# Attention and two MoE layers in one kernel: scores in quarter tiles, mask on VectorE, one ScalarE pass for PReLU, a reordered prologue with filler matmuls

## The chip, the cores and the metric

The kernel runs on one NeuronCore of one Trainium2 chip. The metric is the device time of one execution in microseconds (us); lower is better. Engine names are those of the profile: PE is TensorE (matmuls), PEld its weight loads, DVE is VectorE, ACT ScalarE, POOL GpSimd, SP the engine whose queue issues the loads.

## The reference

Three stages follow each other on 2304 tokens (4 sequences of 576).

```python
scores = scale * q @ k.T                      # 8 heads of 64, window of 64 keys, causal
mask = (rel >= 0) & (rel < 64)
scores = where(mask, scores, -1e9); attn = softmax(scores); x = attn @ v
h = x @ w_in                                  # 512 -> 2048
g = maximum(h, 0) + alpha * minimum(h, 0)     # PReLU, one alpha per column
x = g @ w_out                                 # 2048 -> 512
e = argmax(x @ w_gate); out = gate * relu(x @ w1[e]) @ w2[e]   # 8 experts, one per token
```

All matrix products have float32 accuracy: the large ones split each operand into a high part that one fast pass takes exactly (type fp32r) and a low remainder, and sum three products (high·high, low·high, high·low).

## The kernel before

**Attention.** 18 tiles of 128 tokens with two halves of 4 heads each make 36 groups `g`. A group goes through these steps, each a function and a letter of the table `PLAN`: `X` loads its queries, keys and values (704 KB); `S` (`qk`) computes the scores; `x` (`mx`) takes the row maximum and scales it on DVE; `e` (`ex`) takes four exponentials of 128 columns on ACT with their row sums; `r`, `n` normalize on DVE; `T` transposes on PE; `P` copies the transposed block out of PSUM on ACT; `O` (`pv`) multiplies by the values; `H` and `L` write the high part (ACT) and low part (DVE) of the result, the input of the next stage. Within a tile a query attends to at most 128 keys per half tile of 64 queries. `qk` uses a block layout: four matmuls (one per head) of 128 rows by 128 columns, in which the stationary operand holds the two half tiles of queries in the two diagonal 64 by 64 blocks and zeros elsewhere. The scores fill one PSUM bank of 4 × 128 columns, and the mask is added on PE: two bf16 matmuls of the identity with a table of 0 and -3e38 (`masks`) open the accumulation.

**PReLU layer (MoE 1).** The tokens form 5 blocks, of 4, 4, 4, 3 and 3 tiles, and the 2048 columns 16 chunks `f`. For each block and chunk: `s` (`s1`, 12 matmuls of 512 columns in the blocks of four tiles) gives `h` in PSUM; ACT makes `relu(h)` in a tile `g` (`act_pos`, letter `g`) and `relu(-h)` in place in PSUM (`act_neg`, `R`); DVE combines them to `g - alpha * relu(-h)` (`act_sum`, `t`); ACT and DVE split the result (`h`, `l`); `u` (`s2`, 12 matmuls) accumulates into one PSUM bank per tile (`acc0` to `acc3`). The weights come as raw 1 MB loads, one per chunk (`W`, `load_w`), from 64-bit words and are converted once: steps `0` (ACT), `1`, `2`, `3` (DVE), `4` (ACT), `5` (DVE).

**Routing and experts.** Rows of the finished block are dotted with the gate (`Z`, `N`, `D`), ranked (`G`, `J`, `j`, `M`) and entered into a list (`I`, `i`); afterwards 20 to 25 slots of 128 tokens run through their expert.

**Order.** From the start to the end of the fourth block the order is written by hand in `PLAN` (line 29): a sequence of tokens, letter and number, that `play` turns into instructions. Every engine executes its instructions in that order, so an instruction that waits holds all behind it on the same engine. Groups 0 to 7 (block 0) come first, in the prologue, with their scores in the banks `acc0` to `acc3`; then `s0` begins the steady state, in which groups 8 to 15 run between the chunks of block 0, groups 16 to 23 between those of block 1, and so on. From group 8 on `S`, `T`, `O` and the routing share two rotating banks, tag `att`. Loads go through SP in order, at most eight at a time in flight.

The scores in the code before:

```python
for a in range(2):
    PE.matmul(out=b[:, 2 * a:2 * a + 2, :], lhsT=ident16, rhs=masks(g), start=(a == 0), stop=False)
for u in range(4):
    a, e = divmod(u, 2)
    PE.matmul(out=b[:, u, :], lhsT=q[:, u, :], rhs=k[:, a, 64 * e:64 * e + 128], start=False, stop=(u == 3))
```

Of the kernel before, what the change touches and what calls it, by code (L numbers as in the profile page):

```python
# [42 lines left out]
g18 R18 D9 t18 u17 D10 h18 D11 x17 N4 s20 l18 e17 D12 D13 D14 u18 g19 r17 R19 n17 t19 D15 h19 T17 D16 N5 S18 P17 l19
O17 D17 g20 u19 R20 D18 X19 H17 t20 L17 h20 D19 s21 l20 N6 x18 D20 e18 u20 D21 D22 D23 g21 r18 R21 N7 n18 s22 t21 D24
h21 D25 T18 l21 S19 P18 D26 g22 D27 O18 R22 x19 u21 H18 X20 t22 e19 L18 D28 s23 D29 h22 r19 l22 n19 u22 D30 g23 R23
D31 t23 G0 h23 T19 s24 P19 O19 l23 J0 H19 X21 u23 j0 g24 R24 s25 L19 t24 S20 M0 h24 s26 l24 x20 g25 R25 e20 t25 u24
h25 r20 n20 I0 S21 l25 M1 g26 u25 R26 t26 x21 h26 e21 I1 l26 s27 i0 r21 n21 T20 g27 u26 P20 R27 t27 h27 O20 l27 T21
H20 X22 u27 P21 L20 O21 S22 H21 X23 L21 s28 x22 e22 s29 g28 r22 n22 R28 t28 T22 S23 P22 h28 O22 x23 s30 l28 H22 X24
e23 L22 u28 g29 r23 n23 R29 t29 h29 T23 s31 l29 P23 g30 R30 t30 u29 h30 O23 l30 S24 g31 X25 H23 u30 x24 R31 L23 e24
t31 s32 h31 r24 n24 l31 u31 g32 R32 t32 h32 s33 Z4 l32 Z5 N8 Z6 N9 Z7 u32 g33 R33 D32 D33 D34 T24 D35 s34 P24 t33 N10  # L50
D36 h33 D37 O24 l33 D38 s35 g34 X26 H24 D39 R34 D40 N11 L24 u33 t34 D41 h34 D42 D43 S25 l34 N12 s36 D44 g35 R35 D45
t35 D46 h35 u34 D47 x25 N13 D48 e25 s37 D49 l35 D50 g36 r25 R36 u35 n25 t36 D51 h36 D52 N14 T25 D53 s38 P25 l36 D54
g37 R37 D55 t37 O25 N15 D56 h37 u36 X27 H25 D57 D58 L25 S26 l37 D59 g38 u37 R38 x26 t38 e26 D60 s39 D61 D62 h38 r26
l38 s40 n26 g39 D63 R39 t39 G1 h39 u38 T26 S27 P26 l39 g40 O26 x27 R40 u39 t40 H26 X28 e27 L26 J1 s41 h40 j1 s42 l40
# [26 lines left out]
def attn_moe_moe_kernel(  # L81
# [22 lines left out]

    def f32(ap):
        return ap.bitcast(FP32)
# [19 lines left out]
    nalpha = const.tile([128, 16], FP32, name="nalpha")  # L126
# [5 lines left out]
    def load_consts(i):  # L132
        if i == 0:
            SP.dma_start(out=c16, in_=cst16.bitcast(BF16))
            return
        SP.dma_start(out=c[:, 0:C_I128], in_=cst[:, 0:C_I128])
        SP.dma_start(out=c[:, C_I128:], in_=cst[:, C_DESC:])

    def prep_consts():
# [5 lines left out]
        DVE.tensor_scalar(out=nalpha, in0=alpha, scalar1=-1.0, scalar2=None, op0=ALU.mult)  # L145
# [66 lines left out]

    xt = {}
# [20 lines left out]
    def abank(g=NBT * 2):  # L234
        return bank(f"acc{g % 4}", 1) if g < 2 * BLOCKS[0][1] else bank("att", 2)

    def masks(g):
        i = g // 2
        if (2 * i) % 9 == 0:
            return c16[:, 4:6, :]  # L240
        if (2 * i + 1) % 9 == 0:
            return c16[:, 3:5, :]
        return c16[:, 3, :].unsqueeze(1).to_broadcast([128, 2, 128])

    def qk(g):
        q = raw[g][:, 0:512].rearrange("p (u q) -> p u q", u=4)
        k = raw[g][:, 512:896].rearrange("p (a k) -> p a k", a=2)
        b = abank(g).rearrange("p (u k) -> p u k", u=4)
        for a in range(2):
            PE.matmul(out=b[:, 2 * a:2 * a + 2, :], lhsT=ident16, rhs=masks(g), start=(a == 0), stop=False)  # L250
# [277 lines left out]
    def r_list(j, h=0):  # L528
        n = BLOCKS[j][1]
        if h == 0:  # L530
            lbs[j] = rbank(j)
# [475 lines left out]
```

## Time and profile before

| what | value |
|---|---|
| median of 3 runs | 794.11 us (793.66 to 794.26) |
| the profiled execution | 793.48 us, its span 791.7 us |
| PE busy | 760.3 us, 96% of the span |
| DVE busy | 609.9 us, 77% |
| ACT busy | 496.2 us, 63% |
| POOL busy | 63.5 us, 8% |
| mean granted PE clock | 0.988 of full |

The span runs from the first to the last instruction; 1.8 us of the execution lie outside it. Busy times are for engines that work at the same time, so they don't add up. A PE that is nearly always busy means that its own instruction stream sets the time in those stretches; the stretches where it isn't are to be looked at one by one. In the timeline a row gives the modelled length of a matmul; the distance from start to start tells what it costs in a stream.

### The profile page before, as it was taken

Reading aid. Unit: us, or ns where it says so; the run is one execution under the profiler, and the core shown is the slowest. Engines: PE = TensorE matmul, PEld = TensorE weight load, DVE = VectorE, ACT = ScalarE, POOL = GpSimd, SP = SyncE. Lnnn points to the kernel's source line nnn. Section 1 sums busy time; section 2 is a strip of 40 time slices with the busy share of each in tenths; the row PEclk is TensorE's granted clock in tenths of the full one; section 3 lists DMA queues with packets and bytes.
Section 4 is the critical chain, followed back from the end, with each engine's and each line's share of the span. In section 5 each row is a group of like instructions: output and inputs, shape, how many; then the busy total and the mean of one; then the engine's idle time right before and its main releaser. Section 6 shows DMA issues by size and latency. Waiting matters only on the chain.

```text
span 791.7 us, 12097 instructions
## 1 busy us (share of the span) xinstructions
PE 760.3 (96%) x4284; PEld 634.6 (80%) x4284; DVE 609.9 (77%) x1210; ACT 496.2 (63%) x966; POOL 63.5 (8%) x50
## 2 busy tenths in 40 slices
PE   5589999999999999999999999999999999999995
PEld 4468888888888888888888889887778888888884
DVE  5699898488544786535885486689999999999997
ACT  4687656535344534335354434587888998989986
POOL 0000000000000000000000001011222221221222
PEclk9879999999999999999999999999999999999998
DMA  9981432223221323112222123532066157767521
GB/s 365 407 325 43 144 114 87 74 77 112 93 72 57 98 70 121 38 37 80 87 88 91 67 78 127 222 127 74 27 235 271 54 190 314 237 265 255 192 87 49
DMA packets 24256, 109.86 MB, mean 139 GB/s; under 512 B 3006, under 2 KB 3390, under 8 KB 17024
## 3 DMA queue, kind: packets, MB, share of 16 engines
q1 hardware_dynamic: 20672, 98.25, 34.1%
q0 software_dynamic: 3520, 10.80, 4.0%
q8 instruction: 35, 0.57, 0.3%
q14 instruction: 29, 0.24, 0.1%
HBM read 154.09 MB, written 10.26 MB: 208 GB/s over the span
## 4 chain that ended last, share of the span: by engine, by line
PE 85%; DVE 7%; DMA 5%; issue 2%; ACT 0%; SPq 0%; DVEq 0%; ACTq 0%
PE acc L700 11%; PE h L336 9%; PE acc L383 9%; PE h L338 8%; PE h L337 8%; PE acc L384 8%; PE acc L385 8%; PE h L672 4%; PE h L674 4%; PE h L673 4%; DVE hl L784 4%; PE att L253 3%; PE att L312 2%; DMA hl<-in_wcat_dram 2%; DMA hl<-in_qkv_dram 2%
## 5 line engine op out<-in xcount | busy, mean ns | idle before, releaser
L784 DVE TENSOR_TENSOR hl<-hl,hl 128x1024 fp32r<-128x1024 f32 x176 | 211.2, 1223 | 14.8 <-ACT hl L778 14.1
L778 ACT CAST hl<-hl 128x1024 fp32r<-128x1024 f32 x176 | 180.3, 1049 | 3.9 <-DMA hl<-in_wx_dram 2.3
L700 PE MATMUL acc<-hl,xl 128*128 128x512 f32 x504 | 130.7, 400 | 2.4 <-DVE xl L687 2.4
L336 PE MATMUL h<-xh,hl 128*128 128x512 f32 (+1 forms) x320 | 121.3, 379 | 0.0
L338 PE MATMUL h<-xh,hl 128*128 128x512 f32 (+1 forms) x320 | 118.1, 369 | 0.0
L337 PE MATMUL h<-xl,hl 128*128 128x512 f32 (+1 forms) x320 | 117.8, 368 | 0.0
L384 PE MATMUL acc<-hl,gl 128*128 128x512 f32 x288 | 112.8, 392 | 0.0
L385 PE MATMUL acc<-hl,gh 128*128 128x512 f32 x288 | 112.8, 392 | 0.0
L383 PE MATMUL acc<-hl,gh 128*128 128x512 f32 x288 | 109.9, 401 | 0.1
L700 PEld LDWEIGHTS acc<-hl,xl 128*128 128x128 f32 x504 | 91.2, 188 | 21.4 <-DVE xl L687 3.7
L354 ACT ACTIVATE g<-h 128x512 f32<-128x512 f32 (+1 forms) x80 | 44.5, 557 | 93.3 <-DVE gl L365 57.9
L648 POOL DMA_INDIRECT gx<-x1d,ixg x23 | 39.8, 1729 | 712.5 <-PE acc L385 486.6
L365 DVE TENSOR_TENSOR gl<-g,gh 128x512 fp32r<-128x512 f32 (+1 forms) x80 | 50.9, 636 | 48.4 <-PE acc L384 39.9
L358 DVE SCALAR_TENSOR_TENSOR g<-h,nalpha,g 128x512 f32<-128x512 f32 (+1 forms) x80 | 55.6, 695 | 39.0 <-ACT h L351 38.9
L298 ACT CAST gh<-g 128x512 fp32r<-128x512 f32 (+1 forms) x80 | 46.3, 579 | 58.3 <-DVE g L358 55.2
L439 DVE SCALAR_TENSOR_TENSOR dot<-stage,wge 128x512 bf16<-128x512 f32 x96 | 66.0, 688 | 2.1
L672 PE MATMUL h<-hl,xh 128*128 128x512 f32 x168 | 67.6, 403 | 0.0
L336 PEld LDWEIGHTS h<-xh,hl 128*128 128x128 f32 x320 | 60.3, 188 | 8.6 <-DVE g L358 0.3
L337 PEld LDWEIGHTS h<-xl,hl 128*128 128x128 f32 x320 | 60.3, 189 | 7.8
L338 PEld LDWEIGHTS h<-xh,hl 128*128 128x128 f32 x320 | 60.1, 188 | 7.9
L674 PE MATMUL h<-hl,xh 128*128 128x512 f32 x168 | 66.0, 393 | 0.3 <-DVE xh L660 0.2
L673 PE MATMUL h<-hl,xh 128*128 128x512 f32 x168 | 65.5, 390 | 0.0
(171 smaller groups left out, 1141.2 us busy)
## 6 DMA issues: line engine op xcount, KB each, us to landing
hl<-in_wx_dram SPq DMA_DIRECT2D x92, 1024.0 KB
raw<-in_qkv_dram SPq DMA_DIRECT2D x31, 704.0 KB
hl<-in_wcat_dram SPq DMA_DIRECT2D x14, 1024.0 KB
wge<-in_wgt_dram SPq DMA_DIRECT2D x24, 256.0 KB
hl<-in_qkv_dram SPq DMA_DIRECT2D x5, 704.0 KB
x1d<-stage SPq DMA_DIRECT2D x3, 1032.0 KB
x<-in_wcat_dram SPq DMA_DIRECT2D x2, 1024.0 KB
gx<-in_wgt_dram SPq DMA_DIRECT2D x8, 256.0 KB
```

The costliest lines, as they stand in the source:

```text
L336: PE.matmul(out=h[:, 0:n], lhsT=w_in_op(f, k, 0), rhs=xh[:, k, :], start=(k == 0), stop=False)
L337: PE.matmul(out=h[:, 0:n], lhsT=w_in_op(f, k, 0), rhs=xl[:, k, :], start=False, stop=False)
L338: PE.matmul(out=h[:, 0:n], lhsT=w_in_op(f, k, 1), rhs=xh[:, k, :], start=False, stop=(k == 3))
L383: PE.matmul(out=a, lhsT=gh[:, c0:c0 + 128], rhs=w_out_op(f, 0), start=(f == 0), stop=False)
L384: PE.matmul(out=a, lhsT=gl[:, c0:c0 + 128], rhs=w_out_op(f, 0), start=False, stop=False)
L385: PE.matmul(out=a, lhsT=gh[:, c0:c0 + 128], rhs=w_out_op(f, 1), start=False, stop=(f == 15))
L672: PE.matmul(out=o, lhsT=th[:, k, :], rhs=wh, start=(k == 0), stop=False)
L673: PE.matmul(out=o, lhsT=th[:, k, :], rhs=wl, start=False, stop=False)
L674: PE.matmul(out=o, lhsT=tl[:, k, :], rhs=wh, start=False, stop=(k == 3))
L700: PE.matmul(out=o, lhsT=x[:, f % 4, :], rhs=w[:, lo, (f % 2) * 512:(f % 2) * 512 + 512], start=(x is th and f == 0 and lo == 0), stop=(x i ...
L778: ACT.copy(out=t[:, 0, :], in_=r)
L784: eng.tensor_tensor(out=t[:, 1, :], in0=r, in1=f32(t[:, 0, :]), op=ALU.subtract)
```

## The change

- **Scores in quarter tiles.** `qk` issues eight matmuls of 64 rows (contraction) by 64 output rows by 128 columns instead of four full ones: for each head pair `a` and each `e`, one per half tile `r`, on the four quadrants of the array in turn. The two half tiles write to two PSUM banks, 256 columns of each. Groups 0 to 7 use pairs of `acc` banks. From group 8 on a group's scores take both `att` banks, which are now handed out by a list (`aslot`, `give`): scores give them back after the exponentials, transposes after `P`, values after `L`.
- **Mask.** Groups 0 to 15 keep the mask as two bf16 matmuls, one per bank. From group 16 on (`LATE`, 20 half tiles) DVE adds it in PSUM before the maximum, two instructions of 256 columns.
- **Small steps.** The maximum is two reductions; its scaling (`y`) and the addition of 1e-9 to the sums (`q`) are steps of their own, on POOL where the token ends in `p` (the groups 2 to 15), else on DVE. Six `P` copies of the prologue go to DVE (`P0d` to `P5d`), three normalizations (`n8a` to `n10a`) to ACT.
- **PReLU.** `act_pos` is gone. ACT writes `relu(-h)` to the tile `g`, and DVE computes `g * (1 - alpha) + h` with `h` from PSUM.
- **Prologue.** A new `PLAN`; tokens `b` and `B` issue filler matmuls on bf16 data (8 on zeros, 47 on the constants, 512 columns each) whose results are not read.
- **Lists.** `r_list` closes its accumulation for each pair of tiles, each followed by its own `r_add`.

```diff
 PLAN = """
-c0 X0 W0 S0 c1 X1 x0 e0 10 X2 C0 00 r0 W1 S1 n0 20 T0 P0 S2 x1 X3 30 O0 e1 x2 X4 11 H0 r1 W2 n1 e2 S3 L0 T1 x3 S4 P1
...
+c0 X0 b8 X1 c1 S0 X2 B2 x0 S1 y0 C0 e0 W0 B7 x1 y1 e1 S2 q0 r0 X3 n0 x2 T0 B2 P0d y2p X4 00 q1 O0 r1 n1 e2 10 T1 X5 S3
...
+    attb = [bank("att0", 1), bank("att1", 1)]
+    idle = [0, 1]
+    held = {}
+    def aslot(who):
+        i = idle.pop(0)
+        held.setdefault(who, []).append(i)
+        return attb[i]
+    def give(who):
+        idle.extend(held.pop(who, []))
...
+    LATE = 2 * BLOCKS[2][0]
...
+    def busy(n, x=None):
+        x = c16[:, 0:4, :].rearrange("p a b -> p (a b)") if x is None else x
+        b = bank("h", 2)
+        for _ in range(n):
+            PE.matmul(out=b, lhsT=x[:, 0:128], rhs=x, start=True, stop=True)
...
-        for a in range(2):
-            PE.matmul(out=b[:, 2 * a:2 * a + 2, :], lhsT=ident16, rhs=masks(g), start=(a == 0), stop=False)
-        for u in range(4):
-            a, e = divmod(u, 2)
-            PE.matmul(out=b[:, u, :], lhsT=q[:, u, :], rhs=k[:, a, 64 * e:64 * e + 128], start=False, stop=(u == 3))
+        if g < 2 * BLOCKS[0][1]:
+            two = [bank(f"acc{2 * (g % 2) + r}", 1) for r in range(2)]
+        else:
+            two = [aslot(("S", g)) for r in range(2)]
+        b = [z[:, 0:256].rearrange("p (a k) -> p a k", a=2) for z in two]
+        added = g >= LATE
+        for r in range(0 if added else 2):
+            PE.matmul(out=b[r], lhsT=ident16, rhs=masks(g).unsqueeze(1).to_broadcast([128, 2, 128]),
+                      start=True, stop=False)
+        for a in range(2):
+            for e in range(2):
+                for r in range(2):
+                    h = slice(64 * r, 64 * r + 64)
+                    PE.matmul(out=b[r][64 * e:64 * e + 64, a, :], lhsT=q[h, 2 * a + e, h], rhs=k[h, a, 64 * e:64 * e + 128],
+                              start=added, stop=(added or a == 1))
...
-        DVE.tensor_reduce(out=nm, in_=sm[g], axis=AX.X, op=ALU.max, negate=True)
-        DVE.tensor_scalar(out=nm, in0=nm, scalar1=0.125, scalar2=None, op0=ALU.mult)
+        for r in range(2):
+            if g >= LATE:
+                m = masks(g).unsqueeze(1).to_broadcast([128, 2, 128])
+                DVE.tensor_tensor(out=sm[g][r], in0=sm[g][r], in1=m, op=ALU.add)
+        for r in range(2):
+            DVE.tensor_reduce(out=nm[:, r, :], in_=sm[g][r], axis=AX.X, op=ALU.max, negate=True)
...
-        ACT.activation(out=hb[j, f], in_=hb[j, f], func=ACTF.Relu, scale=-1.0)
...
-        DVE.scalar_tensor_tensor(out=g, in0=hb.pop((j, f)), scalar=nalpha[:, f:f + 1], in1=g,
-                                 op0=ALU.mult, op1=ALU.add)
+        ACT.activation(out=g_tile(j, f, "g"), in_=hb[j, f], func=ACTF.Relu, scale=-1.0)
...
+        DVE.scalar_tensor_tensor(out=g, in0=g, scalar=beta[:, f:f + 1], in1=hb.pop((j, f)), op0=ALU.mult, op1=ALU.add)
```

The order of instructions shows two places. On PE, the scores of group 16, early in block 1, between the matmuls of `u` and `s` (names are output<-inputs, rows by columns of the output). Before:

```order
L250 LDWEIGHTS c_68
L250 MATMUL att<-c_68 128x256
L250 LDWEIGHTS c_68
L250 MATMUL att<-c_68 128x256
L253 MATMUL att<-raw 128x128 x4
```

Now:

```order
L279 MATMUL att_67<-raw 64x128
L279 MATMUL att_68<-raw 64x128
L279 MATMUL att_67<-raw 64x128
L279 MATMUL att_68<-raw 64x128
L279 MATMUL att_67<-raw 64x128
L279 MATMUL att_68<-raw 64x128
L279 MATMUL att_67<-raw 64x128
L279 MATMUL att_68<-raw 64x128
```

The two mask matmuls are gone, and eight quarter matmuls alternate between the two banks `att_67` and `att_68`.

On DVE, the prologue from the maximum of group 7 on: `L180` (after the change `L195`) is step `1` of a weight chunk, the first instruction of DVE that needs its load, and `hl_288`, `hl_317`, `hl_367` are chunks 3, 4 and 5. Before:

```order
L258 TENSOR_REDUCE nm<-acc_307 128x4
L259 TENSOR_SCALAR nm<-nm 128x4
L180 TENSOR_SCALAR hl_288<-hl_288 128x1024
L275 TENSOR_SCALAR rs<-ss 128x4
L276 RECIPROCAL rs<-rs 128x4
L325 TENSOR_TENSOR xl<-att,xh 128x2x128
L280 TENSOR_TENSOR sm<-sm,rs 128x512
L180 TENSOR_SCALAR hl_317<-hl_317 128x1024
L196 TENSOR_TENSOR hl_355<-hl_95,hl_355 128x2x512
L275 TENSOR_SCALAR rs<-ss 128x4
L276 RECIPROCAL rs<-rs 128x4
```

Now, with `hl_257` and `hl_352` the chunks 1 and 2:

```order
L290 TENSOR_REDUCE nm<-acc_435 128x2
L290 TENSOR_REDUCE nm<-acc_436 128x2
L364 TENSOR_TENSOR xl<-att_68,xh 128x2x128
L337 COPY pt<-att_67 128x512
L313 RECIPROCAL rs<-rs 128x4
L321 TENSOR_TENSOR sm<-sm,rs 128x512
L195 TENSOR_SCALAR hl_257<-hl_257 128x1024
L199 SCALAR_TENSOR_TENSOR hl_257<-hl_257 128x1024
L203 SCALAR_TENSOR_TENSOR hl_257<-hl_257 128x1024
L364 TENSOR_TENSOR xl<-att_68,xh 128x2x128
L313 RECIPROCAL rs<-rs 128x4
L321 TENSOR_TENSOR sm<-sm,rs 128x512
```

Up to the low part `L` of group 7 (the eighth `L325`, now the eighth `L364`) DVE had seven instructions of step `1` ahead, for chunks 0 to 6, and nine of the steps `2`, `3`, `5`; now it has three of step `1`, for chunks 0 to 2, and eight of the others.

## Rows read from the trace of the kernel before

**Rows 1.** Page, the span and part 1 (us, share, instructions).

```profile
span 791.7 us, 12097 instructions
...
PE 760.3 (96%) x4284; PEld 634.6 (80%) x4284; DVE 609.9 (77%) x1210; ACT 496.2 (63%) x966; POOL 63.5 (8%) x50
```

**Rows 2.** By stretch: its length, busy us of each engine, PEclk, DMA share, GB/s.

```profile
0.00:48.10 48.10, 28.33 (x251) 23.16 (x252) 32.12 (x69) 28.59 (x91) 0.40 (x6) 0.86 0.94 372
40.00:50.00 10.00, 6.53 (x41) 5.53 (x40) 9.85 (x14) 8.54 (x10) 0.00 (x0) 0.58 0.79 298
300.00:400.00 100.00, 100.00 (x596) 85.33 (x596) 58.31 (x160) 43.79 (x124) 0.00 (x0) 1.00 0.22 73
```

**Rows 3.** Waits of PE after 48 us: total us, times, longest us.

```profile
PE acc L700 <- DVE xl L687: 2.4, 3, 1.4
```

**Rows 4.** Chain of waits, 0 to 60 us (start us, us, what).

```profile
22.59 15.38 DMA hl<-in_wcat_dram
...
37.99 0.69 DVE hl L180
```

**Rows 5.** Timeline of PE, start of the program (start us, us).

```profile
5.81 2.08 PE L253 MATMUL acc<-raw 128*128 128x128 f32 x8 [1.93 <-DMA raw<-in_qkv_dram]
...
28.82 1.16 PE L253 MATMUL acc<-raw 128*128 128x128 f32 x8 [1.53 <-DMA raw<-in_qkv_dram]
...
47.71 0.77 PE L336 MATMUL h<-xh,hl 128*128 128x512 f32 x1
...
48.55 0.39 PE L338 MATMUL h<-xh,hl 128*128 128x512 f32 x1
```

**Rows 6.** Timeline of PE, scores of group 9 between block-0 matmuls.

```profile
53.34 0.39 PE L338 MATMUL h<-xh,hl 128*128 128x512 f32 x1
53.56 0.39 PE L250 MATMUL att<-c 128*128 128x256 bf16 x2
53.79 1.06 PE L253 MATMUL att<-raw 128*128 128x128 f32 x8
54.61 0.47 PE L336 MATMUL h<-xh,hl 128*128 128x512 f32 x1
54.92 0.39 PE L337 MATMUL h<-xl,hl 128*128 128x512 f32 x1
```

**Rows 7.** Timeline of PE, probabilities times values of group 8.

```profile
71.30 0.39 PE L385 MATMUL acc<-hl,gh 128*128 128x512 f32 x1
71.61 0.69 PE L312 MATMUL att<-pt,raw 128*64 128x64 f32 x16
72.23 0.50 PE L336 MATMUL h<-xh,hl 128*128 128x512 f32 x1
72.56 0.39 PE L337 MATMUL h<-xl,hl 128*128 128x512 f32 x1
```

**Rows 8.** DVE instructions by line, 0 to 48.1 us (busy us, mean ns).

```profile
L280 DVE TENSOR_TENSOR sm<-sm,rs 128x512 f32<-128x512 f32 x8 | 5.5, 691 | 0.4
L258 DVE TENSOR_REDUCE nm<-acc 128x4 f32<-128x512 f32 x8 | 5.5, 689 | 12.3 <-PE acc L253 12.2
L184 DVE SCALAR_TENSOR_TENSOR hl<-hl 128x1024 int32<-128x1024 int32 x4 | 4.9, 1222 | 0.0
L180 DVE TENSOR_SCALAR hl<-hl 128x1024 int32<-128x1024 int32 x7 | 4.8, 691 | 2.2 <-DMA hl<-in_wcat_dram 2.2
...
L325 DVE TENSOR_TENSOR xl<-att,xh 128x256 fp32r<-128x256 f32 x8 | 3.3, 415 | 0.0
...
L259 DVE TENSOR_SCALAR nm<-nm 128x4 f32<-128x4 f32 x8 | 1.4, 170 | 0.3
```

**Rows 9.** Timeline of DVE, the last low part before the steady state.

```profile
47.89 0.42 DVE L325 TENSOR_TENSOR xl<-att,xh 128x256 fp32r<-128x256 f32 x1
```

**Rows 10.** Timeline of ACT, exponentials of group 0 and what follows them.

```profile
8.92 0.37 ACT L267 ACTIVATE sm<-acc,nm 128x128 f32<-128x128 f32 x1 [6.67 <-DVE nm L259]
...
10.31 1.14 ACT L176 ACTIVATE hl<-hl 128x1024 f32<-128x1024 f32 x1
```

More of the change, by code (lines that the diff above doesn't have):

```diff
@@ L134, in load_consts @@
             SP.dma_start(out=c16, in_=cst16.bitcast(BF16))
+            DVE.tensor_copy(out=c16[0:64, 5, :], in_=c16[0:64, 4, :])
+            DVE.tensor_copy(out=c16[0:64, 4, :], in_=c16[0:64, 3, :])
             return
@@ L137, in load_consts @@
         SP.dma_start(out=c[:, C_I128:], in_=cst[:, C_DESC:])
+        POOL.tensor_scalar(out=beta, in0=alpha, scalar1=-1.0, scalar2=1.0, op0=ALU.mult, op1=ALU.add)
     def prep_consts():
@@ L266, in ex, with add_eps @@
         for h in range(4):
-            ACT.activation(out=s[:, h, :], in_=x[:, h, :], func=ACTF.Exp, bias=nm[:, h:h + 1], scale=0.125,
+            ACT.activation(out=s[:, h, :], in_=x[h // 2][:, h % 2, :], func=ACTF.Exp, bias=nm[:, h:h + 1], scale=0.125,
                            accum_out=ss[:, h:h + 1])
+        give(("S", g))
         sm[g] = s
         nrm[g] = ss
+    def add_eps(g, eng=DVE):
+        rs = att.tile([128, 4], FP32, tag="rs", bufs=3, name="rs")
+        eng.tensor_scalar(out=rs, in0=nrm[g], scalar1=1e-9, scalar2=None, op0=ALU.add)
+        nrm[g] = rs
     def recip(g):
-        ss = nrm[g]
-        rs = att.tile([128, 4], FP32, tag="rs", bufs=3, name="rs")
-        DVE.tensor_scalar(out=rs, in0=ss, scalar1=1e-9, scalar2=None, op0=ALU.add)
-        DVE.reciprocal(out=rs, in_=rs)
-        nrm[g] = rs
-    def norm(g, eng=DVE):
-        eng.tensor_tensor(out=sm[g], in0=sm[g], in1=nrm.pop(g).unsqueeze(2).to_broadcast([128, 4, 128]), op=ALU.mult)
+        DVE.reciprocal(out=nrm[g], in_=nrm[g])
+    def norm(g, eng=DVE):
+        s, rs = sm[g], nrm.pop(g)
+        if eng is ACT:
+            for h in range(4):
+                ACT.activation(out=s[:, h, :], in_=s[:, h, :], func=ACTF.Copy, scale=rs[:, h:h + 1])
+            return
+        eng.tensor_tensor(out=s, in0=s, in1=rs.unsqueeze(2).to_broadcast([128, 4, 128]), op=ALU.mult)
     def trans(g):
         s = sm.pop(g)
-        b = bank("att", 2)
+        b = aslot(("T", g))
         for h in range(4):
             PE.transpose(b[:, h * 128:h * 128 + 128], s[:, h, :], ident)
-        pT[g] = b.rearrange("p (u q) -> p u q", u=4)
+        pT[g] = b
     def trans_out(g, eng=ACT):
         t = att.tile([128, 4, 128], FP32, tag="pt", bufs=2, name="pt")
-        copy(eng, t, pT[g])
+        copy(eng, t.rearrange("p h q -> p (h q)"), pT[g])
+        give(("T", g))
         pT[g] = t
     def copy(eng, out, in_):
-        if eng is POOL:
-            POOL.tensor_tensor(out=out, in0=in_, in1=one32.unsqueeze(2).to_broadcast(list(in_.shape)), op=ALU.mult)
-            return
         (eng.copy if eng is ACT else eng.tensor_copy)(out=out, in_=in_)
@@ L399, in rbank @@
     def rbank(j):
-        return pbank("att") if j >= NB - 1 else bank("att", 2)
+        return pbank("att") if j >= NB - 1 else aslot(("R", j))
     def r_trans(j, t, tag="xs"):
@@ L493, in r_place @@
         DVE.tensor_tensor(out=rr, in0=rk, in1=oh, op=ALU.mult)
+        give(("R", j))
         rf = small("m", [])
@@ L528, in r_list @@
     def r_list(j, h=0):
-        n = BLOCKS[j][1]
-        if h == 0:
-            lbs[j] = rbank(j)
-        for t, a, bm in ab.pop(j):
-            PE.matmul(out=lbs[j][:, 0:NCOL], lhsT=bm, rhs=a, start=(t == 0), stop=(t == n - 1))
+        lbs[j] = rbank(j)
+        some = ab.pop(j)
+        for i, (t, a, bm) in enumerate(some):
+            PE.matmul(out=lbs[j][:, 0:NCOL], lhsT=bm, rhs=a, start=(i == 0), stop=(i == len(some) - 1))
     lbs = {}
@@ L566, in small @@
             return e2.tile([128] + shape, dt, bufs=1, tag=own, name=nm, **pad)
-        b = pbank("att") if part else bank("att", 2)
+        b = pbank("att") if part else aslot(("R", NB))
         PE.matmul(out=b[:, 0:NE], lhsT=one16, rhs=ohsum, start=True, stop=True)
@@ L574, in slot_table @@
         DVE.tensor_copy(out=nb, in_=ni)
+        give(("R", NB))
         yield
@@ L815, in attn_moe_moe_kernel @@
     with tc.manual_schedule():
+        POOL.memset(zero16, 0.0)
         POOL.memset(one32, 1.0)
```

117 lines of the change are left out of this document (57 added, 60 removed).

## Prediction

> **What bounds the kernel now.** I first read the page: the span is 791.7 us and PE is busy for 760.3 of it, 96% [rows 1]. So nearly everywhere the PE stream itself sets the time, and the question is where it does not. The busy times by stretch answer that: from 300 to 400 us PE is busy all 100 us, DVE 58.31 and ACT 43.79, while in the first 48.1 us PE has 28.33 [rows 2]. PE's waits after 48 us come to little: the longest kind is 2.4 us in three waits [rows 3]. Two things can therefore be won: PE time anywhere after the prologue, at its full worth, and an earlier start of the steady state.
>
> What bounds the prologue? Its chain of waits is a string of loads up to 38 us; the last, 15.38 us from 22.59 on, is that of weight chunk 5, on which step `1` of that chunk (the DVE piece at 37.99) waits and holds all of DVE behind it [rows 4]. The timeline of PE gives the ends: scores of group 0 at 5.81, those of group 7 at 28.82 (after its load), the first matmul of `s0` at 47.71, and at 48.55 the third one, from which on PE doesn't stop [rows 5]. The clock granted between 40 and 50 us is 0.58 of full [rows 2], so the first matmuls of `s0` run slowly too. Counted at full speed (227 ns from start to start, below), `s0` in effect began at 48.55 - 2 × 0.227 = 48.1 us, with the scores of group 8 already behind it.
>
> The profiled execution took 793.5 us, 0.6 below the median of the runs shown, 794.1. The sum is made against the profile and 0.6 added at the end. A measurement of this kernel can tell about 0.2%, 1.6 us, from no change.
>
> **Scores of a group, in the steady state.** One group before: the last `s` matmul starts at 53.34 and costs 0.227, so scores begin at 53.56; the mask takes until 53.79; the next stream matmul but one starts at 54.92, so the whole ends at 54.92 - 0.23 = 54.69 [rows 6]. That is 1.13 us, 0.23 of it mask and 0.90 the eight passes of four matmuls, 0.113 a pass of 128 columns.
>
> For quarter matmuls the trace of before has no row. The nearest is `O`, which already uses the array in column halves: it runs from 71.30 + 0.227 = 71.53 to 72.56 - 0.23 = 72.33, 0.80 us [rows 7]. Its 16 passes have 64 columns, half of 0.113, so one after another they would need 0.90; they start within 72.23 - 71.61 = 0.62. So the two column halves work at the same time: 8 × 0.056 = 0.45 us, and the other 0.35 is what entering and leaving the split array costs. Bounds for the new scores, 16 passes of 128 columns:
> - only column halves overlap: 8 × 0.113 + 0.35 = 1.25 us;
> - all four quadrants overlap: 4 × 0.113 + 0.35 = 0.80 us.
>
> Nothing in the rows excludes that row halves overlap as column halves do, and the change puts them on separate banks, so that the two writes don't meet; I take 0.80 and keep 1.25 as a rival. The Trainium skill (TensorEngine Tiling (Array Packing), Tiling Modes) lists a 64 by 64 split as four tiles that load weights and multiply independently; by that the lower value holds and the sum below is 782, by the pairs alone that these rows show it is 795. No row here shows four at once.
>
> - Groups 16 to 35, without mask on PE: 1.13 - 0.80 = 0.33 each, 20 × 0.33 = **-6.6 us**.
> - Groups 8 to 15, with the mask (0.23): 1.13 - 1.03 = 0.10 each, **-0.8 us**.
>
> **What hides the rest.** The mask on DVE is two instructions of 256 columns at about 0.415 (the low part `L`, from PSUM, has that size), with the split maximum about 1.0 us more per group on an engine that is busy 58 of 100 us [rows 8, 2]: less than eight groups in that stretch bring it to about 66%, so it costs nothing unless someone waits for it. ACT loses a pass of `h` per chunk; nothing on PE waits for ACT there, so it gains nothing by itself; it shortens the way from `s` to `u`. The lists' extra additions are small DVE work, covered by PE. The fillers only matter where they stand in front of something due: 47 × 0.227 = 10.7 us of PE at full clock, in a prologue where PE has 48.1 - 28.3 = 19.8 us to spare [rows 2]; 32 of them (7.3 us) stand between the scores of group 7 and `s0`, up to seven in a row (1.6 us). That could delay `s0` by up to 3 us, and goes into the range. In return the clock stays up, which is in the 48.1 above.
>
> **The prologue.** DVE is the engine to count. Up to the end of the last `L` of block 0 (47.89 + 0.42 = 48.31 [rows 9]) it is busy 32.12 + 0.21 = 32.3 us and idle 16.0: 7.9 before its first maximum, which follows the scores of group 0 (5.81 + 2.08 [rows 5]), and 8.1 afterwards, of which 12.3 - 7.9 = 4.4 on scores and 2.2 on weight loads [rows 8]. By the order of instructions its work ahead of that `L` changes so, with the means of rows 8:
> - four steps `1` fewer, 4 × 0.691, and one of the long steps fewer, 1.22: -4.0;
> - six scalings and six additions to POOL, 12 × 0.17: -2.0;
> - the maximum in two halves, at 2 × 0.415 instead of 0.689, eight times: +1.1;
> - six copies of `P`, 512 columns, as 0.691 of `n`: +4.1; small constants +0.2.
>
> Together -0.6: the work stays 31.7 us. What goes is waiting: chunks 3 to 5 are no longer asked of DVE before `s0`, and group 7 is loaded before chunk 2. With quarter scores the first maximum can start at about 7.0 (half of the 2.08 saved, at the low clock). If DVE never idled again the last `L` would end at 7.0 + 31.7 = 38.7; with all 8.1 us of idle it would be 46.8. I take 2.5 us of idle, nearer the first, since the loads were the chain's main part: 41.2. `s0` began 0.6 before the end of that `L`; so 40.6, say 41.0 with a filler in front. The scores of group 8 now come after it, 1.03, so the point to set beside 48.1 is 42.0: **-6.1 us**, between -9.0 and -0.9. POOL's small steps have no row of their kind: as cheap as DVE's 0.17 at the best, and at the worst the two of group 7, which nothing covers, add some 3 us, inside the same bounds.
>
> **Two banks for one group.** Between the scores of a group from 8 on and the end of its exponentials neither the next scores nor a transpose can start. The way through is two masks and two maxima (4 × 0.415), a scaling of 0.17 and four exponentials, 10.31 - 8.92 = 1.39 us [rows 10]: 3.2 us. Between the scores of group 17 and the transposes of group 16 the new plan has `s19` and `u17`, 24 × 0.227 = 5.45 us. That leaves 2.2 us for whatever stands ahead on DVE and ACT. I take 28 groups × 0.05 = **+1.5 us** of PE standing; bounds 0 and the rival below.
>
> **Sum:** -6.6 - 0.8 - 6.1 + 1.5 = -12.0: 793.5 - 12.0 = 781.5, and with the 0.6 of the median **782.1 us**.
>
> **Rivals.**
> - *Quarters overlap only in pairs.* Then a group costs 1.25 (groups 16 to 35: +0.12 × 20 = +2.4) or 1.48 with the mask (8 × 0.35 = +2.8), with the prologue and the standing as above: +0.6, 794.7 us. For it: rows 7 show pairs and no more. Against: nothing ties the row halves. Chance 0.15.
> - *The change makes PE wait for the two banks (slower).* Place: between scores and the next transposes or scores in blocks 0 to 3. Price: 28 groups × w on top of -13.5; it decides the sign from w = 0.54 us (over +1.6) and at w = 0.8 gives +8.9, 803.0 us. For it: only 2.2 us of reserve in queues that carry five other kinds of work, and the exponentials, which free the banks, stand behind both. Against: DVE and ACT have over a third of their time free there. The Trainium skill (TensorEngine Tiling (Array Packing), PSUM Bottleneck) warns that splitting the array speeds up TensorE and not the emptying of PSUM; here that would be this rival, 803 us. The traces so far show PE waiting 2.4 us in all on such a thing. Chance 0.12.
> - *The prologue is not shortened*, because DVE idles as before, now behind POOL, ACT or fillers: `s0` at 46.2, gain 0.9 with the scores of group 8 behind it, sum -0.9 - 7.4 + 1.5 = -6.8: 787.3 us. Chance 0.10.
>
> **Numbers.** Main case 0.63, from 776 (short prologue, no standing, half of the 0.35 of switching saved for some groups) to 788 (prologue 3 us late, more standing). The range to hold 8 in 10 takes in the late prologue and the pairs: 775 to 795; left out are most of the slower rival and little else. Faster by over 0.2%: 0.63 + 0.10 + 0.03 of the pairs = 0.76. Within 0.2%: 0.10, nearly all pairs. Slower: 0.12 + 0.02 = 0.14.
>
> **What would show it.** Right: eight quarter matmuls within about 0.5 us and 0.8 from stream matmul to stream matmul; `s0` near 41 us at full clock; PE without gaps of more than a few tenths up to 500 us; the rest as before. Wrong: 16 passes over more than 0.9 us; idle PE ahead of transposes or scores that ends with an exponential or a `give`; `s0` after 45 us with DVE idle behind POOL; fillers just before a transpose that was ready.

## The result and the profile after

The changed kernel takes 780.64 us (median of 4 runs, 780.53 to 780.84); the kernel before, on the same chip, 793.88 (793.53 to 794.26). The ratio is 0.983, with a 95% interval of 0.9818 to 0.9843: faster by 1.7%, 13.2 us. The forecast was 782.1 in a range of 775 to 795. The profiled execution took 780.53 us, its span is 778.7, which stands against 791.7 [rows 1].

Page of the changed kernel: the span, part 1 (busy us, share, instructions), and two rows of the 40 slices.

```profile
span 778.7 us, 12731 instructions
...
PE 759.4 (98%) x4590; PEld 611.9 (79%) x4595; DVE 622.6 (80%) x1267; ACT 461.3 (59%) x892; POOL 76.6 (10%) x80
...
PE   8999999999999999999999999998999999999996
...
PEclk9999999999999999999999999999999999999998
```

By stretch of the changed kernel, the three stretches of [rows 2] (length; busy us of PE, PEld, DVE, ACT, POOL; PEclk, DMA share, GB/s):

```profile
0.00:48.10 48.10, 42.55 (x414) 25.44 (x420) 37.83 (x76) 31.86 (x91) 4.48 (x21) 1.00 0.98 391
40.00:50.00 10.00, 9.79 (x57) 7.33 (x56) 7.68 (x10) 7.56 (x16) 0.58 (x2) 1.00 1.00 416
300.00:400.00 100.00, 99.24 (x685) 82.39 (x684) 67.21 (x192) 37.16 (x109) 0.00 (x0) 1.00 0.27 90
```

PE is busy 42.55 instead of 28.33 us in the first 48.1, at the full 2.4 GHz (1.00) where 40 to 50 us had 0.58 before. Of the 42.55 us, 17.6 are filler matmuls, so the busy share alone doesn't show an earlier start; the row of `s0` below does. In the middle DVE has risen from 58.3 to 67.2 of 100 us, and PE still leaves only 0.76 idle. The DMA share is 1.00 between 40 and 50 us: what is scarce there has changed, and that comes back below.

Timeline of PE in the changed kernel: scores of group 0 and of group 7, then the first and the third matmul of `s0` (start us, us):

```profile
5.44 1.05 PE L279 MATMUL acc<-raw 64*64 64x128 f32 x16
...
26.52 0.67 PE L279 MATMUL acc<-raw 64*64 64x128 f32 x16
...
38.65 0.58 PE L376 MATMUL h<-xh,hl 128*128 128x512 f32 x1
...
39.30 0.39 PE L378 MATMUL h<-xh,hl 128*128 128x512 f32 x1
```

Against [rows 5], `s0` starts at 38.65 instead of 47.71. Counted as the prediction counts, it began in effect at 39.30 - 2 × 0.227 = 38.85, and with group 8's scores of 1.03, which now come later, the point to set beside 48.1 is 39.9. The last low part of DVE ahead of it, against [rows 9]:

```profile
38.93 0.42 DVE L364 TENSOR_TENSOR xl<-att,xh 128x256 fp32r<-128x256 f32 x1
```

Scores of group 16 in the changed kernel, as [rows 6] show those of group 9 before:

```profile
147.99 0.39 PE L378 MATMUL h<-xh,hl 128*128 128x512 f32 x1
148.31 0.67 PE L279 MATMUL att<-raw 64*64 64x128 f32 x16
148.91 0.50 PE L376 MATMUL h<-xh,hl 128*128 128x512 f32 x1
149.24 0.40 PE L377 MATMUL h<-xl,hl 128*128 128x512 f32 x1
```

From 147.99 + 0.227 = 148.22 to 149.24 - 0.227 = 149.01 it is 0.80 us, where 1.13 was. All 20 groups without a mask on PE take 0.798 to 0.809; with the mask it is 1.034. In the single records the 16 passes start in four waves of four, 6 to 7 ns apart within a wave; the second wave starts 160 ns after the first, the later ones 109 ns apart. In the kernel before, one full pass of 128 columns took 111 to 112 ns. So the four passes of a wave take the time of one, and four quadrants work at once.

Waits of PE from 41 us to the end (total us, times, longest us), against [rows 3]:

```profile
PE acc L737 <- DVE xl L724: 2.5, 3, 1.4
PE att L351 <- ACT pt L337: 1.7, 3, 0.7
PE h L376 <- DVE g L395: 0.8, 2, 0.6
...
PE acc L419 <- DVE gl L401: 0.4, 1, 0.4
```

The first row, in the expert phase, stood there before. The other three are new. From 40 us to the last `u` PE idles 3.0 us (463.30 - 460.29), where it idled 0.3 (467.70 - 467.41) over the same chunks before. The two stretches, of the changed kernel and of the kernel before (columns as above):

```profile
40.00:503.30 463.30, 460.29 (x2923) 375.87 (x2922) 334.12 (x827) 198.23 (x505) 12.34 (x18) 1.00 0.29 102
```

```profile
48.10:515.80 467.70, 467.41 (x2732) 394.94 (x2732) 321.23 (x771) 230.67 (x573) 2.05 (x2) 1.00 0.28 96
```

**Where the 13.0 us of span went.** Batches of attention matmuls are measured from stream matmul to stream matmul as above:

| part | forecast, us | measured, us |
|---|---|---|
| effective start of `s0`, with group 8 behind it | -6.1 | 48.1 to 39.9: -8.2 |
| scores of groups 16 to 35 | -6.6 | 20 × (0.798 - 1.132) = -6.7 |
| scores of groups up to 15, mask on PE | -0.8 | 7 × (1.034 - 1.132) = -0.7 |
| two `O` in a row, four times | none | 4 × (1.281 - 2 × 0.815) = -1.4 |
| PE standing, from 40 us to the last `u` | +1.5 | 3.0 - 0.3 = +2.7 |
| other joints between batches, and the rest | none | +1.7 |
| from the last `u` to the end | none | -0.5 |
| sum (before rounding) | -12.0 | -13.0 |

The row of 1.7 is what remains. About 0.8 of it can be named: in the kernel before, five times an `O` stood directly ahead of scores, 1.841 us for both instead of 0.815 + 1.132 (0.5 in all), and nine times transposes, scores and an `O` stood together at 2.366 instead of 2.391 (0.2). Those neighbours are gone. The other 0.9 isn't assigned.

### The profile page after: what moved, and what is told of

Its sections match the earlier page's. It is cut to its first block, busy times and chain, and to the rows that moved or that the text cites. A ratio compares the mean times of both kernels' runs of the same rounds, so it can differ in the third digit from the quotient of the medians.

```text
span 778.7 us, 12731 instructions
## 1 busy us (share of the span) xinstructions
PE 759.4 (98%) x4590; PEld 611.9 (79%) x4595; DVE 622.6 (80%) x1267; ACT 461.3 (59%) x892; POOL 76.6 (10%) x80
## 4 chain that ended last, share of the span: by engine, by line
PE 81%; DVE 9%; DMA 6%; issue 2%; ACT 1%; SPq 0%; DVEq 0%
PE acc L737 12%; PE h L376 8%; PE acc L418 8%; PE acc L419 8%; PE acc L420 8%; PE h L377 8%; PE h L378 8%; DVE hl L819 4%; PE h L709 4%; PE h L711 4%; PE h L710 4%; DMA hl<-in_wcat_dram 2%; PE att L351 2%; DMA hl<-in_qkv_dram 2%; PE att L279 2%
## 5 line engine op out<-in xcount | busy, mean ns | idle before, releaser
L685 POOL DMA_INDIRECT gx<-x1d,ixg x23 | 39.9, 1734 | 567.8 <-DVE ixg L682 345.7
L337 ACT CAST gh<-g 128x512 fp32r<-128x512 f32 (+1 forms) x80 | 46.5, 581 | 45.9 <-DVE g L395 42.8
L395 DVE SCALAR_TENSOR_TENSOR g<-g,beta,h 128x512 f32<-128x512 f32 (+1 forms) x80 | 55.0, 688 | 16.3 <-ACT g L391 16.1
```

## The experiments

All are edits of the changed kernel. Beside each time stands the ratio to the kernel before with its 95% interval, to be held against 0.983. The changed kernel was timed in another session than the edits, and the kernel before reads 793.9 to 794.9 us in these sessions, so a difference of two times can be off by as much as 1 us; the ratios are the safer measure.

### Is it the quarters, and are there four at once?

**Full scores again.** Four full matmuls over one bank, the mask on PE, one maximum of 512 columns; everything else as changed.

```diff
-        for a in range(2):
-            for e in range(2):
-                for r in range(2):
...
+        for a in range(2):
+            PE.matmul(out=b[:, 2 * a:2 * a + 2, :], lhsT=ident16, rhs=masks(g), start=(a == 0), stop=False)
+        for u in range(4):
+            a, e = divmod(u, 2)
+            PE.matmul(out=b[:, u, :], lhsT=q[:, u, :], rhs=k[:, a, 64 * e:64 * e + 128], start=False, stop=(u == 3))
```

> One part undone: scores of all groups again as four full matmuls with the mask as two bf16 matmuls on PE, one bank filled (both are still held as in the changed kernel), one maximum over 512 columns; prologue, fillers, PReLU and all else as changed. Theory (the scores' PE time counts in full): groups 16 to 35 cost 1.13 instead of 0.80, groups 8 to 15 1.13 instead of 1.035, 20 x 0.33 + 8 x 0.10 = +7.4 us, 788.0 us. Rival (the gain lies in the prologue alone and the steady state has slack): +0 to +3, 781 to 784 us.

Measured: 788.18 us, 0.9924 (0.9905 to 0.9942), 7.5 us above the changed kernel. `s0` begins at 38.99, so the prologue keeps its gain. The quarters and the move of the mask together are worth 7.5 us and the rest of the change nearly 6, which agrees with the second and third rows of the table.

**Halves outermost; one quadrant twice in a row.** Two other orders of the same 16 passes.

```diff
# halves outermost
+        for r in range(2):
+            for a in range(2):
+                for e in range(2):
# the same quadrant twice
+        for e in range(2):
+            for r in range(2):
+                for a in range(2):
```

> The eight quarter matmuls of a group in another order: both heads' column halves of the first half tile, then those of the second (loop r outermost). Theory (quadrants work at the same time, but a matmul can't start before the one ahead of it in the order): three waves and a half instead of two, a group's scores take about 1.02 us instead of 0.80, 28 groups x 0.22 = +6.3 us, about 787 us. Rival (every quadrant works through its own queue, order is free): 0.80 and 780.6 us.

> The eight quarter matmuls so ordered that each quadrant gets its two matmuls one directly after the other (loop a innermost). Theory (in order): the second matmul holds the next quadrant back, 10 passes of 0.113 one behind the other, a group's scores about 1.48 us, 28 x 0.68 = +19 us, about 800 us. Rival (own queue for each quadrant): 0.80 and 780.6 us.

Measured: 781.95 (0.9842, 0.9826 to 0.9859) and 781.5 (0.9839, 0.9823 to 0.9855). Both expectations fell. The scores of group 16 where the same quadrant is named twice running:

```profile
148.14 0.39 PE L378 MATMUL h<-xh,hl 128*128 128x512 f32 x1
148.46 0.69 PE L279 MATMUL att<-raw 64*64 64x128 f32 x16
149.08 0.50 PE L376 MATMUL h<-xh,hl 128*128 128x512 f32 x1
149.41 0.40 PE L377 MATMUL h<-xl,hl 128*128 128x512 f32 x1
```

From 148.37 to 149.18 it is 0.82 us (median 0.819 over 20 groups; 0.812 with the halves outermost; 0.798 as changed), and the passes still start in waves of four. The records show that the order did change: within a wave the passes start 13 to 14 ns apart here, 7, 20 and 7 ns with the halves outermost, 6 to 7 as changed. So a pass of a free quadrant doesn't wait here for an earlier one of a busy quadrant, and my theory of a strict program order is out. The change's own order is worth 20 × 0.02 = 0.4 us at most, which these times can't tell from nothing.

**Mask on PE everywhere.** VectorE loses its two additions in groups 16 to 35.

```diff
-    LATE = 2 * BLOCKS[2][0]
+    LATE = 2 * NTILE
```

> The mask of groups 16 to 35 goes back to PE as two matmuls before the quarter matmuls; VectorE loses its two additions per group. Theory (PE sets the time in the steady state and VectorE has room): 20 x 0.236 us = +4.7, 785.4 us, with DVE down to about 60 us in 300 to 400. Rival (VectorE's two additions hold the banks long enough to cost PE nearly what they save): +0 to +2, 781 to 783 us.

Measured: 786.4, 0.9897 (0.988 to 0.9913). By the profile the start of `s2` is late by 1.26 us, on a load, with the same instructions up to there; from that point to the last matmul the loss is 4.7 us, the theory's number. DVE's two additions cost PE nothing. So of the 7.5 us of the run with full scores, 4.7 belong to the mask's move to DVE, and the quarter matmuls themselves save 28 × (1.132 - 1.034) = 2.7. Full scores with the mask on DVE were not run; whether the move needs the quarters is not shown.

**Mask on VectorE from group 8 on.**

```diff
-    LATE = 2 * BLOCKS[2][0]
+    LATE = 2 * BLOCKS[1][0]
```

> The mask is added on DVE from group 8 on instead of from 16, two instructions of 0.42 us for each of 8 more groups, and the bf16 mask matmuls are left to the prologue. Theory (DVE has room in block 0): 8 x 0.236 = -1.9 us, 778.8 us. Rival (DVE converts weights there and is 97% busy in the first 30 us of the steady state): PE waits for the low parts, 0 to +3 us, 781 to 784 us.

Measured: 781.3, 0.9835 (0.9817 to 0.9852); no gain. From `s0` to `s16` only 0.5 of the 1.9 us is left. Waits of PE from 38 to 500 us in this run:

```profile
PE h L376 <- DVE g L395: 2.0, 4, 0.8
...
PE acc L419 <- DVE gl L401: 0.4, 1, 0.4
```

Two of the four waits of the first row, 0.73 us at 45.9 and 0.81 at 53.1, lie where DVE still prepares weights (steps `1`, `2`, `3`, `5`, until about 60 us); at these two places the changed kernel waits 0.20 and 0.55. The wait of the second row, at 56.7 us, is new. That makes 1.2 us more before 60 us, which fits the rival: there an addition on DVE isn't covered. But 0.5 of it is the wait ahead of `s2`, which differs as much between runs whose edits lie elsewhere, so the rival is likely and not shown.

### What shortened the prologue

**Weight steps early again.** The steps `1` of chunks 3 to 5 go back ahead of group 7's reciprocal on DVE.

```diff
 PLAN (order on DVE)
+13 14 15 r7
...
-42 13 s0
+42 s0
```

> One part of the order undone: step 1 of the weight chunks 3, 4 and 5 stands again ahead of the normalization of group 7 on DVE, as in the kernel before; the work is the same. In the changed kernel chunk 5 is used by ACT from 38.3 us on and group 7 is normalized at 33.7. Theory (the wait for the load of chunk 5 held the prologue of the kernel before): DVE stands until about 38 us, s0 starts at 43 to 44 instead of 38.65; 1 to 2 us of it come back since the chunks after it are further ahead: +3 to +5 us, 784 to 786 us. Rival (DVE's work alone sets the prologue): s0 at most 1 us later, under 782 us.

Measured: 787.08, 0.9906 (0.9887 to 0.9924): 6.4 us lost, more than I had said. DVE, and the transposes of group 7 that wait for it:

```profile
36.05 0.70 DVE L195 TENSOR_SCALAR hl<-hl 128x1024 int32<-128x1024 int32 x1 [1.74 <-DMA hl<-in_wcat_dram]
38.52 0.69 DVE L195 TENSOR_SCALAR hl<-hl 128x1024 int32<-128x1024 int32 x1 [1.78 <-DMA hl<-in_wcat_dram]
...
39.34 0.69 DVE L321 TENSOR_TENSOR sm<-sm,rs 128x512 f32<-128x512 f32 x1
...
40.08 1.11 PE L327 MATMUL att<-c,sm 128*128 128x128 f32 x4 [6.04 <-DVE sm L321]
...
46.49 0.58 PE L376 MATMUL h<-xh,hl 128*128 128x512 f32 x1
```

Two steps wait 1.74 and 1.78 us for loads, the normalisation of group 7 stands behind them, and PE waits 6.04 us for it. `s0` comes at 46.49, near the 47.71 before. Against the changed kernel the transposes start 5.5 us later (40.08 against 34.60): 3.5 are the two waits, 2.1 the three steps' own work. So the earlier start hangs on this one place in DVE's queue: work that waits for a load no longer stands ahead of work that doesn't. What share this place had in the kernel before is not shown by the run; there the seven steps `1` were spread out, and DVE waited 2.2 us for their loads [rows 8].

**No fillers.**

```diff
 PLAN
-b8 B2 B7 B2 ... B7 B7
```

> All 55 filler matmuls left out; their results are not read, so the output is the same. Theory (they only keep the clock up, and DVE sets the prologue): the clock falls to half in parts of the prologue, the first s matmul comes 0 to 1 us later and the first microseconds of the steady state run slowly: +1 to +3 us, 782 to 784 us. Rival (they stand in the way of due work on PE): s0 1 to 2 us earlier, 779 us.

Left out are 63 matmuls, not 55: the trace of the changed kernel has 63 weight loads of fillers, 8 on zeros and 55 (not 47) on the constants.

Measured: 782.35, 0.9848 (0.9832 to 0.9865), 1.7 us above the changed kernel by the times, 1.4 by the ratios, whose intervals overlap. The stretch from 30 to 40 us of this run, then the first two matmuls of `s0` and the first of `s1`:

```profile
30.00:40.00 10.00, 5.92 (x62) 4.64 (x63) 9.79 (x14) 8.53 (x17) 0.42 (x1) 0.83 1.01 420
```

```profile
37.69 0.80 PE L375 MATMUL h<-xh,hl 128*128 128x512 f32 x1
38.28 0.63 PE L376 MATMUL h<-xl,hl 128*128 128x512 f32 x1
...
42.49 0.50 PE L375 MATMUL h<-xh,hl 128*128 128x512 f32 x1
```

The changed kernel has 9.21 us of PE and a clock of 1.00 there. Without fillers `s0` starts 0.96 us earlier, at 37.69, but its first matmuls run at half clock (0.50 from 37 to 39 us), and `s1` starts as in the changed kernel (42.49 against 42.51); `s8` and `s48` start 0.4 later. So the fillers cost 1.0 us where they stand in front of `s0`, and the full clock gives it back within `s0`. The span of this profile is 2.7 us longer; what goes beyond the 0.4 is lost after `s48`, far from the fillers. A gain of 1.7 us by the fillers is therefore not shown.

**Small steps on VectorE.** The scalings and additions of groups 2 to 15 leave POOL.

```diff
 PLAN
-y2p q2p ... y15p q15p
+y2 q2 ... y15 q15
```

> The 28 scalings and additions that went to POOL are on DVE again. On POOL two of them took 0.53 and 1.00 us in the profile of the changed kernel, on DVE 0.17. Theory (DVE sets the prologue and has no idle to give): 12 steps x 0.1 to 0.17 more on DVE ahead of s0, +1 to +2 us, 782 us. Rival (DVE and ACT wait for POOL's hops): s0 earlier by 1 to 2 us, 779 us.

Measured: 781.23, 0.9836 (0.982 to 0.9853). `s0` is 0.72 us later, at 39.37; of the time 0.6 us is left, too little to be told from no change. In the changed kernel POOL's scalings and additions up to 45 us take 0.23 and 0.26 us on the mean, where DVE's take 0.17.

**The ACT pass twice.** A second pass over `h` for each chunk, 44 us of ACT in all.

```diff
+        ACT.activation(out=g_tile(j, f, "g"), in_=hb[j, f], func=ACTF.Relu)
         ACT.activation(out=g_tile(j, f, "g"), in_=hb[j, f], func=ACTF.Relu, scale=-1.0)
```

> ACT makes two passes over h again for each chunk (one relu whose result is overwritten by the second), 80 x 0.56 = 44.6 us more of ACT. Theory (ACT is covered by PE except in the first chunks, where it waits for weight loads): 0 to +1.5 us, 781 to 782 us. Rival (the pass taken away is a part of the gain): 0.6 us for each of the first 6 to 16 chunks, +4 us or more, 785 us.

Measured: 780.39, 0.9826 (0.9808 to 0.9844), with ACT busy for 504.8 us instead of 461.3. The pass that the change takes away from ACT is no part of its gain.

### The pairs of `O` and the new waits

Two `O` in a row in the changed kernel (groups 18 and 19), to be held against [rows 7]:

```profile
195.59 0.39 PE L420 MATMUL acc<-hl,gh 128*128 128x512 f32 x1
195.91 1.15 PE L351 MATMUL att<-pt,raw 128*64 128x64 f32 x32
196.99 0.50 PE L418 MATMUL acc<-hl,gh 128*128 128x512 f32 x1
197.33 0.39 PE L419 MATMUL acc<-hl,gl 128*128 128x512 f32 x1
```

From 195.82 to 197.10 it is 1.28 us for two, 0.35 less than twice 0.815. That can be had more often, and three waits of PE (0.68, 0.34 and 0.68) can be covered.

**Four more pairs.** Groups 12/13, 16/17, 24/25 and 26/27; for 16/17:

```diff
 PLAN
-T16 q17 N3 r17 l18 s20 P16 n17 R19 D8 D9 O16 ... h19 T17 D13 s21 P17 l19 D14 R20 D15 t20 O17
+q17 N3 r17 l18 s20 n17 R19 D8 D9 ... h19 T16 T17 D13 P16 s21 P17 l19 D14 R20 D15 t20 O16 O17 X18 X19
```

> The plan of the change with four more pairs of groups (12/13, 16/17, 24/25, 26/27) whose transposes stand together and whose O matmuls stand together: the first group's T, P, O, H and L move back to those of the second; nothing is added or taken away. Theory (what a batch of split-array matmuls costs beyond its passes, 0.35 us, lies in entering and leaving the split, so a second batch right behind the first doesn't pay it): 4 x 0.35 = -1.4 us against the changed kernel, 779.2 us, and each new pair of O reads 1.28 us from stream matmul to stream matmul instead of 2 x 0.82. Rival (the 0.35 is in each batch itself): no change, 780.6, or slower where the later transfer of the first group makes the next scores wait.

**And the waits.** 32/33 paired, a chunk ahead of the `O` of 34 and 35, mask of groups 14 and 15 on VectorE.

```diff
-P34 t59 J2 q35 O34 h59 r35 n35 s61 H34
+P34 t59 q35 h59 r35 n35 s61 J2 O34 H34
-T35 P35 t60 O35 M4 h60 s62 H35
+T35 P35 t60 M4 h60 s62 O35 H35
```

> As the run before it, and three things more: groups 32 and 33 are paired too, with a chunk s or u between each transpose and the O that needs its copy (also for 34 and 35), and the mask of groups 14 and 15 goes to VectorE. Theory: one more pair -0.35, the three waits of PE for the PSUM copy in the changed kernel (0.68, 0.34 and 0.68 us at 390, 412 and 418 us) gone -1.7, two masks fewer 2 x 0.23 = -0.5: another -2.5 us, 776.7 us and 3.9 below the changed kernel. Rival: the waits come back elsewhere (an h bank, a score bank), 779 us as the run before.

Measured: 783.39 (0.9861, 0.9844 to 0.9877) and 784.11 (0.9877, 0.9856 to 0.9899): both slower than the changed kernel. All the new pairs take 1.28 us, as expected, and each is paid for. (0.7 us of the first run's loss is the wait ahead of `s2`, 0.95 instead of 0.20, which differs between runs.) In the run of four pairs, PE's waits from 38 to 500 us, then SP and PE around group 18's scores:

```profile
PE att L279 <- DMA raw<-in_qkv_dram: 2.8, 4, 0.9
```

```profile
174.20 0.81 SPq L248 DMA_DIRECT2D raw<-in_qkv_dram x2
...
178.32 0.67 PE L279 MATMUL att<-raw 64*64 64x128 f32 x16 [0.75 <-DMA raw<-in_qkv_dram]
```

A group's load can be issued only when the `O` two groups back has freed its buffer. Pairing delays that `O`, two loads are issued together, and the scores, due 3.4 us later, wait 0.75 for the first. I had allowed for a late transfer between engines and not for the load. In the second run 1.46 us of this kind came at 401 us, and in place of PE's wait for the copy at 418 us there were waits for `t60` (0.68) and for the low part of chunk 60 (0.74): there VectorE was late as well, and the copy had hidden it.

**Two pairs, later scores, and the waits with their other half.** Groups 16/17 and 24/25, with scores 18, 19, 26 and 27 one chunk later; the activation steps of chunk 60 ahead of group 34's `O`.

```diff
 PLAN
-L17 D18 D19 S18 s22
+L17 D18 D19 s22 S18
-q35 O34 h59 r35 n35 s61 H34 l59 L34 R60 j2 u59 T35 P35 t60 O35 M4 h60 s62
+q35 h59 r35 l59 n35 R60 s61 t60 J2 O34 H34 L34 j2 u59 h60 T35 P35 l60 M4 s62 O35
```

> The changed kernel with: groups 16/17 and 24/25 paired as in the run of four pairs, but the scores two groups on stand one chunk later, behind s22 and s38 (and those of 19 and 27 behind s23 and s39), so that their loads have 7.7 us instead of 4.1; a chunk between the transposes and O of groups 32, 34 and 35, with the activation steps that this chunk needs moved ahead; and the mask of groups 14 and 15 on VectorE. Theory (the pairs save 0.35 each, and the run of four pairs lost only by late loads; PE's waits of 0.68, 0.34 and 0.68 us go where another chunk covers the copy): 2 x -0.35 - 1.7 - 2 x 0.23 = -2.9, 777.7 us, a ratio to the kernel before of 0.979 to 0.980, with PE gaps after 60 us of under 1 us in all up to 480 us. The load wait near 46 us, which other runs showed between 0.2 and 1.5 us, can take up to 1 of it. Rival (the chunk put in the way makes the next one wait for its bank or its low part, as in the run with pairs and waits, 0.68 and 0.74 us): 780 us, no better than the changed kernel.

Measured: 779.22 us (778.69 to 780.37), 0.981 (0.9797 to 0.9824). That is 1.4 us below the changed kernel by the times, 1.6 by the ratios, half of what I had expected; the intervals of the two ratios overlap, so it is a likely gain and not a sure one. Its waits of PE from 38 to 500 us, and the one at 398 us:

```profile
PE h L376 <- DVE g L395: 1.3, 3, 0.6
PE att L351 <- ACT pt L337: 0.6, 1, 0.6
PE att L279 <- DMA raw<-in_qkv_dram: 0.6, 1, 0.6
```

```profile
398.31 0.67 PE L279 MATMUL att<-raw 64*64 64x128 f32 x16 [0.64 <-DMA raw<-in_qkv_dram]
```

The pairs (`s16` to `s48` 0.7 us shorter), the mask (0.5 from `s3` to `s16`) and the waits at 412 and 418 us came as forecast. Around group 32 one wait was changed into two others, for the copy of group 33 and for the load of 34, 0.65 and 0.64 us; so PE's gaps from 60 to 480 us came to 1.3 us, where under 1 was expected.

## Why the prediction was right, point by point

The scores, the mask and the direction of the prologue came as forecast, but that the sum was only 1.0 us off is in part luck: errors of -2.1 (prologue), -1.4 (pairs of `O`) and -0.5 (the end) met errors of +1.2 (standing) and +1.7 (other joints).

- **Quarters in four at once, 0.80 us a group:** right; 0.798. Of the two bounds, 0.80 and 1.25, the one that the trace of before had no row for was the true one. Of the 0.33 us that a group saves, 0.23 is the mask and 0.10 the quarters. The Trainium skill (TensorEngine Tiling (Array Packing), Tiling Modes) states four independent tiles for such a split; the waves of four agree with it.
- **The mask and two maxima on DVE cost nothing in the steady state:** right; DVE is busy 67.2 of 100 us (66 was said), and taking the additions away gained nothing. It is right only from about 60 us on, as the run with the mask from group 8 shows.
- **The prologue, -6.1:** the step that was mis-sized most; it measured -8.2. DVE began its first maximum at 6.55 instead of 7.0. Its work from there to the end of the last `L` (39.35) is 31.1 - 0.4 = 30.7 us, where 31.7 was worked out, and it idled 39.35 - 6.55 - 30.7 = 2.1 us, not 2.5. Those three make 1.9 of the 2.1 us. The rest is that `s0` in effect begins 0.5 us ahead of the end of that `L`, where 0.2 was allowed for.
- **Two banks for one group, +1.5 of standing:** the total was too low and the place was wrong. PE stood 2.7 us more than before, and no wait of the list above is one for the two banks. The sign "PE without gaps of more than a few tenths up to 500 us" failed, with gaps of 0.55, 0.68 and 0.68. The first piece is the early one, at 45.7 and 52.9 us: ACT's step `0` waits for weights, and the activation of chunk 0 stands behind it; at 52.9 three weight steps of DVE stand ahead of the combination for chunk 1 as well.

ACT in the changed kernel, with what its waits ended on, and the chain of waits in that time:

```profile
43.29 1.14 ACT L191 ACTIVATE hl<-hl 128x1024 f32<-128x1024 f32 x1 [1.30 <-DMA hl<-in_wcat_dram]
44.33 0.58 ACT L391 ACTIVATE g<-h 128x512 f32<-128x512 f32 x1
...
45.77 1.19 ACT L191 ACTIVATE hl<-hl 128x1024 f32<-128x1024 f32 x1 [0.86 <-DMA hl<-in_wcat_dram]
```

```profile
26.68 19.06 DMA hl<-in_wcat_dram
...
45.77 0.03 ACT hl L191
```

  The chain holds 19.06 us of weight loads up to 45.74, where it held 15.38 up to 37.99 [rows 4]; DMA is at 1.00. What holds the first chunks now is the loads. The wait before `s2` was 0.2 us here and between nothing and 1.5 in the runs of the edits. Its second piece is the `O` that stood directly behind its own transposes at 390 and 418 us, with only the PSUM copy between them.
- **Fillers, up to +3 against:** they are 55 on the constants, 12.5 us, and not 47 with 10.7; the 32 between group 7 and `s0` are counted rightly. They cost 1.0 ahead of `s0`, which the clock gave back by `s1`; a net gain of some tenths is likely, and the 1.7 of the time is not shown to be theirs.
- **ACT's pass, nothing:** right, by the doubled pass. **POOL's steps, 0.17 to 3 us late:** 0.23 and 0.26 each, and DVE would be slower by 0.7 at `s0`.
- **Not foreseen:** -1.4 for `O` in pairs. The prediction had the 0.35 of entering and leaving the split array and saw that half of it "saved for some groups" could lower the range; it didn't count in the new order how often two `O` stand together. With that and the lost neighbours (+0.8) the sum would have been 781.5, at the same prologue.
- **Rivals:** pairs only (1.25 us, 794.7), waits for two banks (803.0), prologue as before (787.3) — each fell on its own row: 0.798 us; no wait on a score bank; `s0` at 38.65.

## What to carry to other kernels

When 64-row matmuls fill a quarter of the array, give the halves their own PSUM banks, as here (one bank for both was not run), and count four passes in the time of one, plus 0.35 us for each stretch of split matmuls; then look in the order how many such stretches can be joined, and ask for each join what stands behind it, here the buffer of the load two groups on. In a prologue, list for each engine's queue the instructions that wait for a load and move those behind everything that waits for compute; three misplaced steps cost 6.4 us here, more than the mask's move (4.7) or the quarters alone (2.7). A wait that is covered may hide a second one behind it: two of the three covered here uncovered another.

## What the runs showed of the hardware that was not expected

- Passes for a free quadrant started ahead of earlier ones of a busy quadrant: with the same quadrant named twice in a row a group took 0.819 us, not the 1.48 that an order kept strictly would have given.
- The 0.35 us belongs to a stretch of split matmuls, not to each `O`: two in a row took 1.281 us, in every one of the pairs that the runs made. In a group's 0.80 us, 0.09 lies ahead of the first pass, 0.60 from the first pass to the next stream matmul, and 0.11 behind that one's start.
- Two loads of 704 KB issued together at 174.20 us in the run of four pairs: the scores that needed the first were due 3.4 us later and started 4.1 us later. In these runs that distance counts and not that two go together: in the changed kernel two are issued 0.46 us apart, at 142.29 and 142.75 us, the scores stand 6.0 us behind the first, and none waited.
